# Releasing the software DMA loads at the first memset instead of at the first cast of q

## The chip, the cores and the metric

The kernel runs on one core of one Trainium2 chip. The metric is the time of the device for one execution, in microseconds, as the median of several runs. The profile is of one execution and has a span of its own (310.0 us here), a little apart from the median.

## The reference

The input is q, k and v of 4 batches, 8 heads, 768 positions and 64 elements per head, and a list of random blocks. Two stages follow each other.

```python
scores = scale * np.matmul(q, k.transpose(0, 1, 3, 2))
# mask: 32x32 blocks; neighbours, first and last row and column of blocks, 3 sampled blocks per row
scores = np.where(mask, scores, -1000000000.0)
attn = softmax(scores)
x = attn @ v                      # then heads side by side: (4, 768, 512)
...
a1 = alpha1 * x + beta1
tok = np.einsum('ts,bsd->btd', w_tok, a1)
u = x + lam * tok
a2 = alpha2 * u + beta2
ch = np.maximum(a2 @ w_ch1, 0.0) @ w_ch2
return u + lam * ch
```

The lines are shortened: the softmax subtracts the row maximum and adds a small constant to the sum. The second stage mixes tokens with a 768x768 matrix and then channels with a 512x2048 and a 2048x512 matrix, each time with a residual.

## The kernel before

**Tiling.** Heads are taken in 16 pairs, (batch, two heads). The scores of a pair are computed transposed, keys on partitions, in 9 units of 1,024 columns, so there are 144 units. For a unit, TensorE computes scores (L729 for the first 6 pairs, with the mask as 24 added rows of q and k; L850 for the rest, two heads side by side on half of the rows of the array), ScalarE takes the exponential into `eT` (L744, L802), and TensorE multiplies by v (L769, L883). The later pairs are masked after the exponential on VectorE (L807). A norm step (L701, L704) writes the result into `x_sb`. After both heads of a pair come the token mixing for the pair's 128 channels (L942 to L978, matmuls at L962) and a transpose into `uT` (L1000 and its copy for the first batch, a DMA transpose later). When a batch has all four pairs, channel mixing follows: `w1b` matmuls (L1044), a relu into `hts` (L1057, L1061), `w2b` matmuls (L1106), an add (L1123) and the store. The weights of the token mixing are transposed on TensorE at L506.

**Order of the work.** The start is written out by hand. The first pair's q and k (`q2f`, `k2f`), the identity for transposes, block indicators and sampled blocks come in on the queues of SyncE and ScalarE (L235 to L245). `warm` is a tile of zeros, set by VectorE at L248; `keep_warm` (L252) multiplies it by itself, so that TensorE isn't idle before the data is there. `first_cast(0)` turns q and k of the first head into bf16 in `rel0`; `transposes` (L294) and copies put them into `qx[0]` and `kx[0]`.

Everything else is ordered by a planner in the kernel's own code. Each piece of work is a `Job` with an engine, a duration, a priority and what it depends on. A loop walks through time, gives each free engine its best ready job, and emits the instruction at that moment. So each engine's instruction list is in the order of the planned times, and `pin_order` keeps it. The planned times are in no instruction: on the chip each engine runs its list in order and waits on semaphores only.

Five constants say where the plan begins. `T0` is the time from which TensorE, ScalarE, VectorE and SyncE are free for planned jobs (L59, L332); `POOL=4800.0` is the same for GpSimd; `dma_free` and `land.free`, both 8000, are the time from which the DMA engines can serve the software loads. A load is expected to land at `max(dma_free, issue + 2300)` plus its transfer time plus 200 (L1309 to L1311), one after the other.

```python
if e == "PE" and not st["ch2"]:
    fill(t - free_at[e] - 60.0)
```

These two lines (L1289, L1290) put fills into the list: where the plan has TensorE idle, up to the first job of the second channel matmul (L1106), `fill` emits matmuls of `warm` of about that length.

**The loads in question.** All casts during a load, that is q, k and v of later pairs and all weights, are issued by GpSimd (`load`, `load_wtk`, `load_bc`, `load_w1`, `load_w2`; L399 to L472), in the order of `LOADS`. Ahead of them stands one small copy on GpSimd (L324) that reads `rel0`. GpSimd runs in order, so no software load is issued before the first cast of q has written `rel0`.

Of the kernel before, what the change touches and what calls it, by code (L numbers as in the profile page):

```python
# [13 lines left out]
BF = mybir.dt.bfloat16  # L14
# [9 lines left out]
NBLK = S // BLK  # L24
# [3 lines left out]
P = 128  # L28
# [17 lines left out]
    "w1 3", "q 5", "k 5", "v 5", "q 6", "k 6", "v 6",  # L46
)
PR = 1
EARLY = ('b0', 'b1')
OLD = True  # L50
MROW = (2, 3, 9)
# [4 lines left out]
COVER = 800.0  # L56
NLD = 6
HOLD = 2
T0 = 6600.0  # L59
MASK_AT = 28  # L60
AHEAD = 13000.0
SCALE = 1.0 / 8.0
# [74 lines left out]
def kernel(  # L137
# [19 lines left out]
    nc = tc.nc  # L157
# [21 lines left out]
    pp = ctx.enter_context(tc.tile_pool(name="persist", bufs=1))  # L179
# [43 lines left out]
    def bank(name, shape, dt=FP):  # L223
        t = ps7[:, :] if name == "b6" else ps6[:, ts(ALL.index(name), 512)]
        if dt != FP:
            t = t.bitcast(dt)
        t = t[:, 0 : int(np.prod(shape[1:]))]
        return t if len(shape) == 2 else t.rearrange("p (o c) -> p o c", o=shape[1])
# [18 lines left out]
    warm = pp.tile([P, 512], BF, name="warm", tag="warm")  # L247
    nc.vector.memset(warm[:], 0.0)  # L248

    def keep_warm(n, w, name="b6"):  # L250
        for _ in range(n):
            nc.tensor.matmul(bank(name, [P, w]), warm[:, 0:P], warm[:, 0:w], start=True, stop=True)  # L252

    def fill(ns):
        free = [x for x in ("b6", "b0", "b1") if slots[x] > 0]
        while ns > 60.0 and free:
            w = min(512, int(ns * 2.4))
            keep_warm(1, w, free[0])
            ns -= w / 2.4 + 3.0

    keep_warm(7, 512)
    keep_warm(2, P)
    for t in vext:
# [16 lines left out]
    rel0 = wk.tile([P, 2, NT, 2 * D], BF, name="rel", tag="rel", bufs=3)  # L280
# [21 lines left out]
    for w in range(2):  # L302
# [12 lines left out]
        out=qx[0][MB, 0:HS], in0=bqs[0][0:NBLK, 0:HS], scalar1=1.0, scalar2=BIG,  # L315
# [4 lines left out]
    for j in range(2, NQB):  # L320
        nc.sync.dma_start(qx[j][MB, :], qx[0][MB, :])

    hold = pp.tile([P, NBLK], BF, name="hold", tag="hold")
    nc.gpsimd.tensor_copy(out=hold[:], in_=rel0[:, 0, 0, 0:NBLK])  # L324

    ACT_COPY = dict(ACT=790.0)
    dma_free = [8000.0]
    SEM = 70.0  # L330
    DRAIN = 166.0
    free_at = dict(NEVER=1e9, NONE=0.0, PE=T0, ACT=T0, DVE=T0, POOL=4800.0, SP=T0)  # L332
    slots = dict(
        **{b: 1 for b in ALL}, ops=1, eT=NET, head=NQB, vext=NV, ld=NLD, rel=3,
        x=NXB, uT=3, hts=2, a1p=2, ub=2, ot=2, w2b=1,
# [589 lines left out]
    for p in range(len(pairs)):  # L925
# [7 lines left out]
        halves = ((0, D), (D, D)) if n == NPAIR - 1 else ((0, P),)  # L933
        pr = PR if n == NPAIR - 1 else 2
        a_jobs = []
# [213 lines left out]
    def can(j):  # L1149
        for t in j.take:  # L1150
            if isinstance(t, tuple):
                opts = t[0]
                ok = False
                if opts is BANKS:
# [3 lines left out]
                    if st["qk"] < NPE * NU:  # L1158
                        opts = BANKS[:2] if st["ch"] else EARLY
                    elif not hold[1] and any(owned.values()):  # L1160
# [19 lines left out]
    hold = [False, False]  # L1180
# [43 lines left out]
            x[0].done = at + 200.0 + x[0].late  # L1224
        dma_free[0] = at

    land.free = 8000.0
    flying = []
    loads = sorted((j for j in jobs if j.xfer is not None), key=lambda j: (j.prio, j.n))
    t = 0.0  # L1230
# [165 lines left out]
```

The softmax here doesn't subtract the row's maximum and nothing guards it: scores larger than these inputs give would overflow.

## Time and profile before

| what | value |
|---|---|
| time, median of 3 runs | 309.87 us (309.76 to 309.95) |
| span of the profiled execution | 310.0 us |
| TensorE busy | 302.7 us (98%) |
| VectorE / ScalarE / GpSimd busy | 207.2 / 206.4 / 52.1 us |
| software queue: data, share of 16 DMA engines | 15.47 MB, 32.7% |
| first software load: issued, time to landing | 4.82 us, 4.2 us |
| first scores (L729) | 7.61 us |
| matmul records of `warm` after 13.4 us | 11, 3.76 us busy |

Busy time of TensorE is the union of its matmuls with their pipelined ends, so it can't tell a matmul that runs from one that waits for the one before it; starts of successive matmuls tell more. The chain that ended last is followed backwards from the end, at each step to what released the instruction. A name with a q (SPq, POOLq) is an engine's sequencer, which issues transfers. Some matmul records are missing: L252 has 36 matmuls on the program's list and 32 records in the trace.

### The profile page before, as it was taken

Reading aid. Unit: us, or ns where it says so; the run is one execution under the profiler, and the core shown is the slowest. Engines: PE = TensorE matmul, PEld = TensorE weight load, DVE = VectorE, ACT = ScalarE, POOL = GpSimd, SP = SyncE. Lnnn points to the kernel's source line nnn. Section 1 sums busy time; section 2 is a strip of 40 time slices with the busy share of each in tenths; the row PEclk is TensorE's granted clock in tenths of the full one; section 3 lists DMA queues with packets and bytes.
Section 4 is the critical chain, followed back from the end, with each engine's and each line's share of the span. In section 5 each row is a group of like instructions: output and inputs, shape, how many; then the busy total and the mean of one; then the engine's idle time right before and its main releaser. Section 6 shows DMA issues by size and latency. Waiting matters only on the chain.

```text
span 310.0 us, 7557 instructions
## 1 busy us (share of the span) xinstructions
PE 302.7 (98%) x3161; PEld 190.1 (61%) x3194; DVE 207.2 (67%) x435; ACT 206.4 (67%) x270; POOL 52.1 (17%) x91
## 2 busy tenths in 40 slices
PE   7999999999999999999999999999999999999995
PEld 3577788766655665565666575566655665555444
DVE  3379898988898886766889696888958730010111
ACT  4699998898798558756855767775858727428000
POOL 4736530301113112131211210120000000000000
PEclk9999999999999999999999999999999999999999
DMA  6999999995563757376285834558020110010121
GB/s 141 182 252 214 211 201 213 161 137 88 77 105 59 137 53 135 54 114 109 61 127 98 123 65 76 94 89 100 3 62 34 27 27 34 34 70 0 48 90 68
DMA packets 47174, 30.81 MB, mean 99 GB/s; under 512 B 27516, under 2 KB 43044, under 8 KB 47140
## 3 DMA queue, kind: packets, MB, share of 16 engines
q0 software_dynamic: 15984, 15.47, 32.7%
q1 hardware_dynamic: 30940, 14.61, 22.2%
q8 instruction: 25, 0.41, 0.6%
q10 hardware_dynamic: 216, 0.24, 0.3%
q14 instruction: 9, 0.07, 0.1%
HBM read 32.04 MB, written 6.33 MB: 124 GB/s over the span
## 4 chain that ended last, share of the span: by engine, by line
PE 95%; DMA 1%; ACT 1%; issue 1%; DVE 0%; SPq 0%
PE ps L1044 27%; PE ps L1106 21%; PE ps L962 10%; PE ps L729 8%; PE ops L883 8%; PE ps L850 7%; PE ops L1106 5%; PE ops L769 4%; PE ps L252 1%; PE ps L294 1%; DMA identb<-ident_c 1%; PE ps L506 1%; PE ps L1000 0%; ACT eT L802 0%; ACT hts L1057 0%
## 5 line engine op out<-in xcount | busy, mean ns | idle before, releaser
L802 ACT ACTIVATE eT<-ps 128x1024 f16<-128x1024 f32 x90 | 86.9, 1022 | 31.3 <-PE ps L850 27.3
L1044 PE MATMUL ps<-uT,w1b 128*128 128x384 bf16 (+1 forms) x512 | 93.1, 326 | 0.1
L1057 ACT ACTIVATE hts<-ps,b1t 128x384 bf16<-128x384 f32 x104 | 60.1, 582 | 37.7 <-PE ps L1044 32.2
L1106 PE MATMUL ps<-w2b,hts 128*128 128x512 bf16 (+1 forms) x293 | 72.4, 373 | 1.5 <-issue 0.2
L807 DVE TENSOR_TENSOR eT<-eT,maskT 128x1024 f16<-128x1024 f16 x90 | 60.3, 686 | 17.5 <-ACT eT L802 17.3
L1044 PEld LDWEIGHTS <-w1b 128*128 128x128 bf16 x512 | 46.3, 98 | 29.0 <-ACT eT L802 1.2
L1106 PEld LDWEIGHTS <-hts 128*128 128x128 bf16 x400 | 36.6, 98 | 36.2 <-issue 2.2
L744 ACT ACTIVATE eT<-ps 128x1024 f16<-128x1024 f32 (+1 forms) x55 | 52.6, 1016 | 7.1 <-PE ps L729 6.9
L883 PEld LDWEIGHTS <-eT 128*128 128x128 f16 x720 | 30.8, 97 | 15.1 <-issue 4.4
L962 PE MATMUL ps<-a1p,wtokT 128*128 128x128 bf16 x576 | 36.6, 219 | 0.0
L883 PE MATMUL ops<-vext,eT 128*128 128x65 f16 x720 | 36.0, 193 | 0.0
L962 PEld LDWEIGHTS <-wtokT 128*128 128x128 bf16 x576 | 33.3, 98 | 2.9 <-issue 0.5
L729 PE MATMUL ps<-qx,kx 88*128 88x512 bf16 (+1 forms) x144 | 33.2, 341 | 0.2 <-ACT kx L318 0.2
L1123 DVE TENSOR_TENSOR ot<-x_sb,ps 128x512 f32<-128x512 f32 (+1 forms) x20 | 13.4, 671 | 28.3 <-PE ps L1106 28.3
L397 POOL COPY held<-flag 1x1 bf16<-1x1 bf16 x24 | 9.4, 393 | 121.2 <-DVE flag L417 121.2
L850 PE MATMUL ps<-qx,kx 64*128 64x512 bf16 (+1 forms) x240 | 25.6, 326 | 0.0
L769 PEld LDWEIGHTS <-eT 128*128 128x128 f16 x432 | 18.6, 98 | 5.1 <-DVE x_sb L704 0.6
L769 PE MATMUL ops<-vext,eT 128*128 128x65 f16 x432 | 20.4, 194 | 0.1
L972 DVE TENSOR_TENSOR x_sb<-x_sb,ps 128x384 f32<-128x384 f32 x32 | 17.5, 549 | 3.9 <-PE ps L962 3.3
L704 DVE TENSOR_TENSOR x_sb<-ops,rcp 128x384 f32<-128x384 f32 x32 | 17.8, 557 | 1.1
L1123 DVE TENSOR_TENSOR ot<-x_sb,ops 128x512 f32<-128x512 f32 (+1 forms) x5 | 3.2, 634 | 22.5 <-PE ops L1106 22.5
L978 DVE TENSOR_TENSOR ub<-x_sb,a_bc 128x384 bf16<-128x384 f32 x32 | 17.6, 550 | 0.1
(68 smaller groups left out, 224.2 us busy)
## 6 DMA issues: line engine op xcount, KB each, us to landing
out_dram<-ot SPq DMA_DIRECT2D x23, 256.0 KB
v<-in_v_dram POOLq DMA_DIRECT2D x16, 192.0 KB, 4.5
q<-in_q_dram POOLq DMA_DIRECT2D x15, 192.0 KB, 3.9
k<-in_k_dram POOLq DMA_DIRECT2D x15, 192.0 KB, 4.7
w1b<-in_moe_w_ch_dram POOLq DMA_DIRECT2D x4, 512.0 KB, 9.2
w2b<-in_moe_w_ch_dram POOLq DMA_DIRECT2D x4, 512.0 KB, 11.8
wtk<-in_moe_w_tok_dram POOLq DMA_DIRECT2D x3, 384.0 KB, 9.2
maskT<-mask_rows SPq DMA_DIRECT2D x14, 72.0 KB
```

Of the source, the lines that this page charges most:

```text
L704: nc.vector.tensor_tensor(out=x_sb[:, s0 : s0 + NT, h * D : (h + 1) * D], in0=op[:, :, 0:D], in1=rcp[:].unsqueeze(2).broadcast_to([P, NT, D]),
L729: nc.tensor.matmul(sps[:, f - u * UN : f - u * UN + w], kx[h][0:KC, ts(jt, P)], qx[h][0:KC, c : c + w], start=True, stop=True,)
L744: nc.scalar.activation(eT[:, c], sps[:, c], AF.Exp, bias=EXPB, scale=SCALE)
L769: nc.tensor.matmul(ops[p, a][:, t * VW : t * VW + D + 1], eTs[p, u][:, ts(i - u * GU, P)], vx[:, a, jt, 0 : D + 1], start=(i % HT == 0), s ...
L802: nc.scalar.activation(eT[:], sps[:], AF.Exp, bias=EXPB, scale=SCALE)
L807: nc.vector.tensor_tensor(out=e, in0=e, in1=maskT[:, u, :].unsqueeze(1).broadcast_to([P, 2, 512]), op=ALU.min,)
L850: nc.tensor.matmul(sps[:, a * 512 + lo : a * 512 + lo + w], kx[sl][r, ts(jt, P)], qx[sl][r, c : c + w], start=True, stop=True,)
L883: nc.tensor.matmul(ops[p, a][:, t * VW : t * VW + D + 1], eTs[p, u][:, a * 512 + c * P : a * 512 + (c + 1) * P], vx[:, a, jt, 0 : D + 1], ...
L962: nc.tensor.matmul(tp[:, j, :], wtokT[:, s, ts(3 * g + j, P)], tl["a1p", p][:, s, :], start=(s == 0), stop=(s == NT - 1),)
L1044: nc.tensor.matmul(hp[:, 0:nc_], w1b[:, dk, ts(f, P)], uTs[b][:, dk, hf * HS : hf * HS + nc_], start=(dk == 0), stop=(dk == 3),)
L1057: nc.scalar.activation(hts[kk][:, f, :], hp[:, 0:HS], AF.Relu, bias=b1t[:, f : f + 1], scale=1.0)
L1106: nc.tensor.matmul(cps[kk, mi][:, 0:w], hts[kk][:, nk, ts(m, P)], w2tile[0][:, nk, lo : lo + w], start=(nk == 0), stop=(nk == 15),)
```

## The change

The copy on GpSimd that holds back the software loads now reads a piece of `warm`, so the loads are released when the first memset is done. It stands right after the memset in the program. The purpose is to have the loads under way while the first head's data still comes in. The planner's constants are set to go with that: GpSimd is free from 1500 instead of 4800, the DMA engines serve software loads from 4300 instead of 8000, and the other engines start planned jobs at 6200 instead of 6600. Rules, priorities and the order of the loads stay.

```diff
+DMA0 = 4300.0
+POOL0 = 1500.0
...
-T0 = 6600.0
+T0 = 6200.0
...
+    hold_ = pp.tile([1, 8], BF, name="hold", tag="hold")
+    nc.gpsimd.tensor_copy(out=hold_[:], in_=warm[0:1, 0:8])
     keep_warm(7, 512)
     keep_warm(2, P)
...
-    hold = pp.tile([P, NBLK], BF, name="hold", tag="hold")
-    nc.gpsimd.tensor_copy(out=hold[:], in_=rel0[:, 0, 0, 0:NBLK])
...
-    dma_free = [8000.0]
+    dma_free = [DMA0]
...
-    free_at = dict(NEVER=1e9, NONE=0.0, PE=T0, ACT=T0, DVE=T0, POOL=4800.0, SP=T0)
+    free_at = dict(NEVER=1e9, NONE=0.0, PE=T0, ACT=T0, DVE=T0, POOL=POOL0, SP=T0)
...
-    land.free = 8000.0
+    land.free = DMA0
```

## Prediction, made before the result was known

> **What bounds the kernel now.** I read the busy shares first, then the chain that ended last, then who waits, then the chain piece by piece. The page opens with the busy times and gives the chain by engine in its fourth part:
>
> ```profile
> PE 302.7 (98%) x3161; PEld 190.1 (61%) x3194; DVE 207.2 (67%) x435; ACT 206.4 (67%) x270; POOL 52.1 (17%) x91
> ...
> PE 95%; DMA 1%; ACT 1%; issue 1%; DVE 0%; SPq 0%
> ```
>
> TensorE is both the busiest engine and 95% of the chain. The busy figure is of pipelined matmuls, so I checked it with the waits of PE alone (us in total, times, longest):
>
> ```profile
> PE ps L252 <- DVE warm L248: 1.2, 1, 1.2
> PE ps L294 <- DMA identb<-ident_c: 0.4, 1, 0.4
> PE ps L729 <- ACT kx L318: 0.2, 1, 0.2
> ```
>
> All three lie in the first 8 us. After that PE runs its list with no wait over 0.2 us to the last matmul, which ends at 306.5; what follows is one add and a store. So the end time is a sum: the start, plus all matmuls on the list at their pace, plus 3.5 us of tail. Whatever is on the list counts in full, and that includes the fills of L252, matmuls of zeros that the planner emits where it thinks that PE would be idle.
>
> The pieces of the chain (start, length, what) give the pace:
>
> ```profile
> 1.69 3.28 DMA identb<-ident_c
> 5.00 0.80 PE ps L294 x6
> 7.61 1.87 PE ps L729 x5
> 10.12 1.01 PE ps L252 x3
> 11.12 0.85 PE ps L729 x3
> 11.98 0.85 PE ps L252 x2
> 40.91 0.87 PE ps L729 x5
> 299.57 3.45 PE ps L1106 x16
> ```
>
> The same five matmuls of L729 (2,048 columns) take 1.87 us at 7.61 and 0.87 us at 40.91: until about 13 us the array runs at half pace. At full pace 16 matmuls of 512 columns take 3.45 us, 0.421 ns per column; two fills of 512 at 11.98 take 0.85 us, twice that. The fills lie in the early part only. This is the table by stage for the instructions of `warm` alone (stretch, its length, PE busy and count):
>
> ```profile
> 13.40:60.00 46.60, 3.76 (x11) 1.38 (x15) 0.00 (x0) 1.00 1.16 210
> 60.00:310.00 250.00, 0.00 (x0) 0.00 (x0) 0.00 (x0) 1.00 0.43 76
> ```
>
> GpSimd, which issues the software loads, is held once at the start, and its first load follows at 4.82:
>
> ```profile
> POOL hold L324 <- DVE rel L289: 4.2, 1, 4.2
> ```
>
> No VectorE, ScalarE or PE instruction waits for a software load anywhere in the profile: the planner knows when they land, and places their readers later. So the loads bound nothing on the chip directly; they shape the order that the planner writes.
>
> **What the Trainium skill says.** "TensorE: Matmul & The Clock Gate", Part 1, has the array at half clock until a window of about 3.4 us has been busy throughout. The trace agrees on the ratio (1.87 against 0.87 us); with the gaps at 4.6 and 7.4 us full pace came only at 13.3. "DMA: Bandwidth & Descriptors", section "Issuing engines are not separate DMA queues", says that transfers from all issuing engines run on the same 16 DMA engines and interleave. The trace of before keeps them apart: software packets first show after 6.2 us, when the load issued at 4.82 begins to move. From 3 to 6.2 us the two hardware queues alone take 62.2% + 9.8% = 72% of the 16 engines. So the early release puts software traffic onto engines that are three quarters full.
>
> **The change, part by part.**
>
> 1. The copy on GpSimd that holds the loads reads `warm` instead of `rel0`. `warm` is set at 0.86 + 0.27 = 1.13 us, the cast ends at 4.54. The copy took 0.26 us, so the first issue moves from 4.82 to about 1.4: 3.4 us earlier. GpSimd is no bound (52 us busy), so this alone is worth nothing on the path.
>
> 2. Contention. Software data moved about 1.5 us after issue (4.82 to 6.2 or later), so now from about 3.0. The transfers for the first head are then still in flight: both casts start near 4.1, and `identb` lands at 4.97, which is what starts the transposes at 5.00. Bounds: nothing, if the hardware packets are nearly done; 0.9 us, if the last 0.9 us before 4.97 are shared evenly and take twice as long. The second halves of q and k are read at 7.30 and 7.58, and the transposes that need them start at 9.27, so about 1 us of delay there is hidden. I take 0.3 us for the start. It goes to the end in full, as PE has no later slack.
>
> 3. Loads land earlier. The total traffic is the same, and part of the 3.4 us is paid in shared time. Between 3 and 8 us before moved about 0.6 MB on hardware queues; 28% of the engines were free for 3.2 us, worth about 0.9 us of full use. So landings should move by 1 to 2.5 us, while the planner (`DMA0` 8000 to 4300) counts on 3.7. Does a reader stall? In the changed order the cast of the first v load follows the mask copy at 8.03 to 8.38. That load landed at 4.82 + 4.2 = 9.0 in before; moved by 1 to 2.5 us that is 6.5 to 8.0. First q: 5.66 + 4.4 = 10.1, now 7.6 to 9.1. First k: 6.37 + 5.6 = 12.0, now 9.5 to 11. Its cast is due after 10.1, so up to 0.9 us of VectorE wait, ahead of the copy of kx for the second head. That copy serves only the fifth unit, whose matmuls ran after 14 us. Hidden.
>
> 4. The constants `DMA0`, `POOL0` and `T0` make no instruction, but the planner writes another order. I compared the built lists. All work is the same: every line but L252 has the same count and shapes of matmuls, and the groups of L850 keep their number (35), so what changing over to them costs stays. The fills do not: before has 14,060 columns, after 19,092. The first 5,944 columns (the warming ones and the three fills at 10.12) are common. What is left: 8,116 in before, of which 1,024 at half pace (the 0.85 us at 11.98), so 7,092 x 0.421 = 2.99 us at full pace. In after 13,148, of which the first 507 fall in the half-pace time, so 12,641 x 0.421 = 5.32 us. Difference +2.33. In the half-pace time after has 517 columns of fill less, about 0.43 us of clock, in which real matmuls advance by half as much: -0.21. Net +2.1 us.
>
> Why more fills? With data there sooner, the token transposes (L506) and the token mixing (L962) move forward, but L1044, the large block of independent work, starts later in the sequence: after unit 49 instead of 45. Most of the added fills stand between units 37 and 48, where the list holds only scores, attention-times-v and little else. There ScalarE's exponentials, about 0.92 us apart in the trace, set the pace; scores and values of a unit need 0.44 + 0.24 us of PE. Whether PE waits there or multiplies zeros is the same for the end: it is PE time without work, and the last 50 us (256 to 306.5) are channel mixing that runs as fast as PE can. Being ahead with attention buys nothing there.
>
> 5. The hold tile shrinks and moves: nothing.
>
> Sum: 309.87 + 2.1 (fills) + 0.3 (start) = 312.3 us.
>
> **The rivals.**
>
> A. A new wait on top. A start later by 0.5 to 0.9 us can leave the window after 9.9 us not busy throughout, with full pace one window later: 3.4 us at half pace, 1.7 us lost. Or VectorE, in order, waits for loads that are 1 to 2 us later than planned and PE runs dry. Either gives about 314.0. For: landings fall short of the plan. Against: the margins of step 3.
>
> B. No change. The fills are paid, but full pace comes one window earlier, since real work reaches PE sooner: -1.7, so 309.87 + 2.1 - 1.7 = 310.3. Against: everything up to 10.9 us is the same sequence with the same gaps.
>
> C. Faster. The exponentials have 1.5 + 0.7 us of idle before the third and fourth unit (10.5 to 13.7); values multiplied early shorten it, and if ScalarE set the end, that would be 309.87 - 2.2 = 307.7. For: ScalarE is busy 43.0 of 46.6 us from 13.4 to 60. Against: PE has no wait there either, and work that it does not do then it must do later.
>
> **How the numbers follow.** The forecast has 0.68, A 0.15, B 0.10, C 0.07. The forecast itself has 310.9 (half of the added fills displace short waits that the lists hide, no contention) to 313.2 (0.9 at the start, a few short waits). The range 310.3 to 314.0 leaves out C and the far ends of A and B. Slower is the forecast and A, 0.83; B is within 0.2%, 0.10; C is faster, 0.07.
>
> **What would show it.** Right: some 30 fills after 13.4 us (before's list has 15), with about 2.3 us more of chain time; still no PE wait after 10 us; the first software issue near 1.4; identb landing between 5.0 and 5.9; last matmul near 309. Wrong: fills in place but the last matmul no later (then before had waits that I took for work), full pace well before 13 us, or PE waits of over 1 us after 14.

## The result, and the profile after

The changed kernel takes 317.71 us (median of 3 runs, 316.7 to 318.15) against 309.87 (309.76 to 309.95): a ratio of 1.0247 [1.0208, 1.0286], slower by 7.8 us. Measured again beside the kernel before (E1) it was 318.54 against 311.64, 1.022 [1.0192, 1.0247], slower by 6.9 us. The first three runs of before lie at the fast end of the 113 that followed (309.53 to 315.16), so the experiments below compare with that second pair. The direction was forecast; the size was 2.4 us, and 317.71 lies above the range. The profiled execution of the changed kernel has a span of 314.9 us (before: 310.0).

Busy times of the engines and the chain by engine, from the page of the kernel after:

```profile
PE 307.7 (98%) x3208; PEld 190.8 (61%) x3208; DVE 209.8 (67%) x438; ACT 204.0 (65%) x267; POOL 52.2 (17%) x91
...
PE 91%; ACT 3%; DMA 3%; DVE 1%; issue 0%; ACTq 0%
```

TensorE is as busy as ever, but its share of the chain fell from 95% to 91%. About 7% of the span now runs through ScalarE, VectorE and transfers, 2% before: time in which TensorE waits. The list of PE's waits (us in total, times, longest) shows only the first part of it:

```profile
PE ps L254 <- DVE warm L250: 1.2, 1, 1.2
PE ps L299 <- DMA identb<-ident_c: 0.9, 1, 0.9
PE ps L299 <- DVE rel L294: 0.7, 1, 0.7
PE ps L1047 <- ACT eT L805: 0.2, 1, 0.2
```

The wait for `identb` grew from 0.4 to 0.9 us, and one for the cast into `rel` is new. The first loads go out where they were meant to. GpSimd's instructions at the start (start, length, engine, line; in brackets the idle time and what ended it):

```profile
1.20 0.18 POOL L265 COPY hold<-warm 1x8 bf16<-1x8 bf16 x1 [0.75 <-DVE warm L250]
1.33 0.84 POOL L402 DMA_DIRECT2D v<-in_v_dram  x1
2.17 0.72 POOL L402 DMA_DIRECT2D q<-in_q_dram  x1
```

The first issue is at 1.33 instead of 4.82, and the first seven software loads land 1.5 to 2.4 us earlier (first v 6.66 instead of 9.02, first q 8.58 instead of 10.03). What it cost is in the chain of the first 15 us, piece by piece:

```profile
0.74 3.07 DMA q2f<-in_q_dram
...
3.83 6.34 DMA k2f<-in_k_dram
...
10.19 0.37 DVE rel L294
...
10.61 0.82 PE ps L299 x6
11.43 1.01 PE ps L254 x3
12.44 0.85 PE ps L732 x3
```

The chain now goes through the second half of the first pair's k. Its cast starts at 10.19, where before it started at 7.58, and the transposes of the second head start at 10.61 instead of 9.27. The two casts from the traces, first before, then after:

```profile
7.58 0.42 DVE L289 CAST rel<-k2f 128x384 bf16<-128x384 f32 x1
```

```profile
10.19 0.36 DVE L294 CAST rel<-k2f 128x384 bf16<-128x384 f32 x1 [1.90 <-DMA k2f<-in_k_dram]
```

Before, the data was there when VectorE came to it; now VectorE stands 1.90 us, and what follows on its list with it. The queues from 3 to 6.2 us in the kernel after (packets, MB, share of the 16 engines) say why:

```profile
q0 software_dynamic: 327, 0.24, 50.4%
q1 hardware_dynamic: 338, 0.23, 32.3%
```

SyncE's queue, which carries `k2f`, moved 588 packets and 0.56 MB in this stretch before, and 338 and 0.23 MB now. Software traffic had nothing there before, and has half of the engines now. ScalarE's queue has 14.2%, 9.8% before.

For the rest of the kernel I took the start of every matmul from the two traces and priced the work on the list at its full-pace length (0.421 ns per column and the like). What is left over is fills and a remainder, that is waits and half pace:

| us, in the profiled execution | before | after | difference |
|---|---|---|---|
| remainder at the first scores | 3.74 | 4.19 | +0.45 |
| remainder at the third unit's scores | 5.33 | 6.65 | +1.3 |
| remainder at the first scores of L850 / L853 (near 74 us) | 7.78 | 8.79 | +1.0 |
| remainder from there to the last matmul | 7.73 | 9.42 | +1.7 |
| all matmuls of `warm` on the list | 5.96 | 8.09 | +2.13 |
| start of the last matmul | 306.24 | 311.08 | +4.84 |

The remainder to 74 us (+1.0), the remainder after it (+1.7) and the fills (+2.1) make the 4.8 us. The fills are what was forecast. The other two parts were not, and the experiments are about them. The execution profiled in E1, with a span of 317.3, is closer to the median: there the remainder at 20 us is 2.55 us above before's (9.45 against 6.90), and the late one 2.2 us; its last matmul starts 7.2 us later than before's.

When full pace comes can be read from the lengths of equal matmuls and from the granted clock that each profile records: at 13.8 us in before (the prediction had read 13.3) and at 13.5 in after. So in this pair of profiles the longer pauses at the start are a cost, and a longer half pace is none.

### The profile page after: what moved, and what is told of

It reads as the page before. It is cut to its first block, busy times and chain, and to the rows that moved or that the text cites. A ratio compares the mean times of both kernels' runs of the same rounds, so it can differ in the third digit from the quotient of the medians.

```text
span 314.9 us, 7624 instructions
## 1 busy us (share of the span) xinstructions
PE 307.7 (98%) x3208; PEld 190.8 (61%) x3208; DVE 209.8 (67%) x438; ACT 204.0 (65%) x267; POOL 52.2 (17%) x91
## 4 chain that ended last, share of the span: by engine, by line
PE 91%; ACT 3%; DMA 3%; DVE 1%; issue 0%; ACTq 0%
PE ps L1047 27%; PE ps L1109 21%; PE ps L965 10%; PE ops L886 8%; PE ps L853 7%; PE ps L732 6%; PE ops L1109 5%; PE ops L772 4%; ACT eT L747 2%; DMA k2f<-in_k_dram 2%; PE ps L254 2%; DMA q2f<-in_q_dram 1%; PE ps L299 1%; ACT eT L805 1%; DVE ot L1126 1%; PE ps L509 1%
## 5 line engine op out<-in xcount | busy, mean ns | idle before, releaser
L1060 ACT ACTIVATE hts<-ps,b1t 128x384 bf16<-128x384 f32 x101 | 58.2, 583 | 43.7 <-PE ps L1047 37.2
L1109 PE MATMUL ps<-w2b,hts 128*128 128x512 bf16 (+1 forms) x320 | 76.5, 374 | 0.0
L810 DVE TENSOR_TENSOR eT<-eT,maskT 128x1024 f16<-128x1024 f16 x90 | 60.7, 686 | 16.8 <-ACT eT L805 16.7
L886 PEld LDWEIGHTS <-eT 128*128 128x128 f16 x720 | 30.2, 97 | 14.1 <-DVE eT L810 2.2
L886 PE MATMUL ops<-vext,eT 128*128 128x65 f16 x720 | 35.4, 193 | 0.2 <-DVE eT L810 0.2
L1126 DVE TENSOR_TENSOR ot<-x_sb,ps 128x512 f32<-128x512 f32 (+1 forms) x20 | 13.4, 672 | 29.8 <-PE ps L1109 29.7
L732 PE MATMUL ps<-qx,kx 88*128 88x512 bf16 (+1 forms) x144 | 32.7, 337 | 0.2 <-ACT kx L323 0.2
L853 PE MATMUL ps<-qx,kx 64*128 64x512 bf16 (+1 forms) x240 | 26.0, 326 | 0.0
L772 PEld LDWEIGHTS <-eT 128*128 128x128 f16 x432 | 18.2, 98 | 5.4 <-DVE x_sb L707 0.7
L1064 DVE TENSOR_SCALAR hts<-ps,b1t 128x384 bf16<-128x384 f32 x27 | 16.6, 616 | 5.0 <-PE ps L1047 3.7
L772 PE MATMUL ops<-vext,eT 128*128 128x65 f16 x432 | 19.9, 194 | 0.0
```

The costliest lines, as they stand in the source:

```text
L732: nc.tensor.matmul(sps[:, f - u * UN : f - u * UN + w], kx[h][0:KC, ts(jt, P)], qx[h][0:KC, c : c + w], start=True, stop=True,)
L772: nc.tensor.matmul(ops[p, a][:, t * VW : t * VW + D + 1], eTs[p, u][:, ts(i - u * GU, P)], vx[:, a, jt, 0 : D + 1], start=(i % HT == 0), s ...
L810: nc.vector.tensor_tensor(out=e, in0=e, in1=maskT[:, u, :].unsqueeze(1).broadcast_to([P, 2, 512]), op=ALU.min,)
L853: nc.tensor.matmul(sps[:, a * 512 + lo : a * 512 + lo + w], kx[sl][r, ts(jt, P)], qx[sl][r, c : c + w], start=True, stop=True,)
L886: nc.tensor.matmul(ops[p, a][:, t * VW : t * VW + D + 1], eTs[p, u][:, a * 512 + c * P : a * 512 + (c + 1) * P], vx[:, a, jt, 0 : D + 1], ...
L1060: nc.scalar.activation(hts[kk][:, f, :], hp[:, 0:HS], AF.Relu, bias=b1t[:, f : f + 1], scale=1.0)
```

## The experiments

Theory one: three costs add up. The early release slows the first head's loads, so TensorE pauses and is later at full pace; the new list has 2.1 us more of planned idle time; and the new list, of equal work, has late waits. Theory two, the rival: only the start counts (a pause, and half pace prolonged), and the order is worth its fills at most. A third: the fills themselves cost. Every run below is 5 to 22 executions beside the kernel before; medians of before are 311.64 to 311.9, and single executions of one kernel spread by 1 to 5 us. "The late remainder" is the remainder from the 24th matmul of L850 to the last matmul: 6.85 us in before, 8.54 in after. It belongs to the order, and not to the start: that stretch takes 218.8 us in before and in all seven other profiles with before's late order (E2, E5, E6, E9, E11, E12, E13), and 220.5 to 221.0 us in the five with after's order (after, E1, E3, E4, E8).

**E1: the changed kernel again.**

> The changed kernel once more, beside the kernel before on the same chip. The profiled spans differ by 4.9 us (310.0 and 314.9), the medians by 7.8 us. My account of the spans: 2.1 us of added fills, 1.0 us of a later start, 1.7 us of small waits of TensorE between 125 and 215 us. If the span tells the change, the time here is before + 5 us (ratio 1.016). If the medians do, it is before + 8 us (ratio 1.025), and 3 us more are to be found outside my account.

318.54 us, 1.022 [1.0192, 1.0247]. That lies between the two sizes that were weighed. The slowdown stands in a second measurement, and its profile shows how the start varies from run to run. Its chain:

```profile
11.86 1.01 PE ps L254 x3
12.87 0.85 PE ps L732 x3
...
14.58 0.85 PE ps L732 x3
```

Three matmuls of L732 take 0.85 us at 14.58, half pace; in the profile after they took 0.45 at 13.91. Full pace came at 13.5 us there, at 17.0 here, later than in before too.

**E2: the release alone.** The constants of before are put back, so all lists but GpSimd's copy are before's.

```diff
-DMA0 = 4300.0
-POOL0 = 1500.0
-T0 = 6200.0
+DMA0 = 8000.0
+POOL0 = 4800.0
+T0 = 6600.0
```

> The early release alone: the planner's three constants are those of before, and every engine's list is that of before but for the copy on GpSimd. Theory (the changed order costs most): only the start is later, identb 0.45 us and the second half of k another 0.6 to 0.9 us, so before + 1.0 to 1.3 us. Rival (contention costs most, all through the loads): before + 4 us or more. Third: the later half of k is hidden here and the time is before + 0.5 us or less.

313.35 us, 1.007 [1.0046, 1.0093]: +1.7, more than the 1.0 to 1.3 of the theory. The chain of its start:

```profile
3.68 6.93 DMA k2f<-in_k_dram
...
10.63 0.37 DVE rel L294
...
11.05 0.82 PE ps L299 x6
11.87 1.01 PE ps L254 x3
12.87 0.85 PE ps L732 x3
13.73 0.85 PE ps L254 x2
```

The same transfer ends the wait, with before's order of work. The pace is another than in after. The table by stage has the granted clock in the third column from the right:

```profile
4.80:8.20 3.40, 1.41 (x15) 0.81 (x14) 1.17 (x3) 1.30 (x3) 2.06 (x4) 1.00 1.14 202
8.20:15.00 6.80, 5.82 (x21) 2.73 (x22) 3.16 (x9) 3.26 (x5) 1.82 (x4) 0.50 1.21 220
```

Full pace was there from 4.8 us and was lost at 8.2, after pauses, until 15.0. The transposes of the second head start 1.8 us later than in before (11.05 against 9.27), and the 120th matmul of the first scores 1.5 us later (62.02 against 60.52): in this profile the later data is the whole cost, and pace adds nothing to it on balance. The late remainder is before's. So the release by itself costs a quarter of the slowdown, all of it at the start.

**E3: the order alone.** The lists of after, with the loads released by the first cast as before.

```diff
-    hold_ = pp.tile([1, 8], BF, name="hold", tag="hold")
-    nc.gpsimd.tensor_copy(out=hold_[:], in_=warm[0:1, 0:8])
...
+    hold_ = pp.tile([P, NBLK], BF, name="hold", tag="hold")
+    nc.gpsimd.tensor_copy(out=hold_[:], in_=rel0[:, 0, 0, 0:NBLK])
```

> The changed order alone: constants and lists of the changed kernel, but the copy on GpSimd reads rel0 after the first cast, as before. Theory: fills 2.1 us and the later waits 1.7 us stay, the start is that of before, so before + 3.8 us; loads that now land 1.5 to 2.5 us later than in the changed kernel add up to 1 us if a list runs into them. Rival (contention costs most): within 1 us of before.

317.99 us, 1.0197 [1.0168, 1.0227]: +6.35, more than expected. The order carries nearly all of it, but this run has a wait of its own, since the list counts on loads that now come late:

```profile
PE ps L297 <- DVE kx L367: 2.2, 1, 2.2
```

Full pace was there from 5.7 us, was lost at 12.6, after this wait, and came back at 19.4. The late remainder is 8.52, as in after: those waits belong to the order, not to the release. The costs of E2 and E3 don't add up to that of after (1.7 + 6.35 against 6.9): each changes the same start, and E3 has its own wait.

**E4: the order of after without fills.** Left out are only matmuls of zeros, which have no part in the result.

```diff
-                if e == "PE" and not st["ch2"]:
-                    fill(t - free_at[e] - 60.0)
```

> The changed kernel with the planner's fills left out (only the hand-written warming matmuls at the start stay); all other instructions and their order are the same. As I predicted: where fills stand TensorE would wait anyway, so it waits instead of multiplying zeros, and the time is the changed kernel's within 1 us. Rival (fills delay real work that was ready): up to 5.6 us less than the changed kernel, as that is the length of the fills left out, or at least the 2.1 us. Risk on the other side: a pause lets the array fall to half pace, and it is slower.

316.44 us, 1.0154 [1.0129, 1.0179]: 2.1 us less than after beside it, where within 1 us was expected and the rival had 2.1 or more. But the remainder grew as the fills went: at the 120th matmul of L732 fills and remainder make 16.24 us, against 16.72 in the profile after, and at the end 25.99 against 26.30 (28.70 in E1). Two of PE's waits:

```profile
PE ps L299 <- DVE rel L294: 3.2, 1, 3.2
...
PE ps L732 <- ACT eT L747: 2.2, 7, 0.4
```

TensorE waits for the exponentials where it multiplied zeros. From 20 us to the 120th matmul of L732, at full pace throughout, fills and remainder together take 5.1 us in E4 and 5.9 in after, E1, E3 and E8: of the 4.9 us of fills that stood there, 4.1 came back as waits. So the fills of the plan are for the most part idle time under another name, and some 0.8 us of them are a cost of their own. The rest of the 2.1 us lies ahead of 20 us or in chance: E4's start has full pace from 4.9 us and half pace from 11.7 to 15.1, and the changed kernel's has half pace to 13.5 or 17.0. How it divides is not shown. The third theory holds for a part at most.

**E5: is it one load?** The release alone, with the second half of k on ScalarE's queue, so that it needn't wait behind the others on SyncE's.

```diff
+    nc.scalar.dma_start(k2f[:, 1, :], pair_ap(k, 0, 0)[:, 1, :])
...
-    nc.sync.dma_start(k2f[:, 1, :], pair_ap(k, 0, 0)[:, 1, :])
```

> Early release with before's constants and order, and the second half of the first k issued on ScalarE's queue right after that queue's other loads, instead of as the sixth load on SyncE's. In the traces with early release that half lands at 10.2 us instead of by 7.6, and VectorE and then TensorE wait for it. Theory (this one late load is most of what the release costs): before + 0.5 us or less, where the release alone gave before + 1.7. Rival (the release slows all first loads, identb too, or disturbs the clock): still before + 1.2 us or more.

313.95 us, 1.0075 [1.0052, 1.0099]: +2.3, a miss. PE's waits, and VectorE's casts in the timeline:

```profile
PE ps L299 <- DMA identb<-ident_c: 1.8, 1, 1.8
PE ps L299 <- DVE rel L294: 1.6, 1, 1.6
```

```profile
11.10 0.36 DVE L294 CAST rel<-q2f 128x384 bf16<-128x384 f32 x1 [2.83 <-DMA q2f<-in_q_dram]
```

In E2 these two waits are 1.7 and 0.8 us. So `identb` is as late as there, and the second half of q is now the last to land, at 11.1, where in E2 it was k's at 10.6. The delay moved to another load. The release slows several of the first loads, and moving one to the other queue didn't help.

**E6, E7: the fills by size, with the release of before.** Only constants of the kernel before change. E6 plans 13,529 columns of fill (before: 14,060), E7 23,963.

```diff
-    dma_free = [8000.0]
-    land.free = 8000.0
+    dma_free = [7000.0]  # E6; E7: 8500.0
+    land.free = 7000.0   # E6; E7: 8500.0 and T0 = 6400.0
```

> Release as before; the planner's constants 7000 for the loads and 6600 for the engines, which give the fewest fill columns among the constants tried: 13,529, against 14,060 before and 19,092 after. Theory one (fills count what TensorE loses early): before - 0.2 us, plus or minus 0.3 for small waits. Theory two (any other order costs about 2 us in late waits, since the fine order of before happens to avoid them): before + 1.5 us or more.

> Release as before; constants 8500 and 6400, which give 23,963 fill columns, 9,903 more than before. Theory one: 9,903 x 0.421 ns = 4.2 us more, so before + 4.2 us, and before + 5.9 us if the late waits of 1.7 us come with it as they did in the changed order. Rival (fill columns have little to do with the time): within 1.5 us of before.

E6: 311.66 us, 0.9998 [0.9969, 1.0026], as expected. E7: 322.89, 1.0341 [1.03, 1.0381], +11.2 where 4.2 to 5.9 were expected. The trace of E7 has the fills at their price, 10.14 us against 5.96, so +4.2. The remainder is 6.8 us larger on top (22.27 against 15.51). The start isn't the reason, as full pace was there from 4.4 us; it was lost only from 62.5 to 65.9, right after the first of these waits of PE (58.7 to 61.8):

```profile
PE ps L294 <- DVE kx L363: 2.9, 1, 2.9
PE ps L962 <- DVE hts L1061: 1.2, 1, 1.2
```

As in after, a list of the same work has waits beside its fills. The fills show at face value in the trace; they don't tell the whole price of an order.

**E8, E9: the start's pauses closed.** E8 is after with two more warming matmuls before the first transposes and two before those of the second head. E9, the control, is before with one more at the start.

```diff
-    keep_warm(7, 512)
+    keep_warm(9, 512)   # E9: keep_warm(8, 512), and only that
...
+                keep_warm(2, 512)
                 tl["h0"] = transposes(
```

> The changed kernel with four more warming matmuls of 512 columns: two at the end of the first nine, where TensorE waits for identb, and two ahead of the transposes of the second head, where it waits for the second half of k. Theory (the pauses let the half pace last longer; in two profiles of the changed kernel full pace came at 13.5 and 17.0 us, with 2.4 us between the spans): 1 to 2 us faster than the changed kernel. Rival (pauses of 1 us do not matter to the clock, its moment is chance): the changed kernel's time within 0.4 us.

> The kernel before with one more warming matmul of 512 columns at the end of the first nine, where TensorE waits for identb (0.43 us at half pace). Control for the changed kernel with its pauses filled, which gained 2.7 us. If longer half pace is a cost of the change (its pauses are longer), before has little to win: 0 to 0.5 us faster. Rival (both kernels start equally cold, and filling would help either): before - 1.5 us or more, and then the clock explains nothing of the difference.

E8: 315.84 us, 1.0123 [1.0079, 1.0167], 2.7 us less than after, though it adds four matmuls. Zeros can't bring the data sooner, so this is won through the pace. The single executions say the same: four with a mean granted clock of 0.999 or 1.0 took 315.63 to 315.94 us, the two at 0.995 318.04 and 318.55. The profile is of the last, in which half pace came back from 13.4 to 16.8 us, so it doesn't show the gain. E9: 311.51, 0.9998 [0.9973, 1.0022], as expected, but for a reason that I had not foreseen. In its profile full pace is there at 5.35 us, and the kernel is 3.2 us ahead until 60 (the 120th matmul of L729 starts at 57.35 instead of 60.52). Then (waits of PE, and the chain from 63 us):

```profile
PE ps L850 <- DMA kx<-rel: 2.1, 1, 2.1
```

```profile
63.96 8.62 DMA kx<-rel
...
72.63 0.61 PE ps L850 x6
73.24 0.66 PE ops L769 x16
73.90 1.71 PE ps L1106 x4
```

The first pair of L850 can't start before its q and k have come through the loads and the DMA transposes. What was gained ahead of it is waited out there, and four matmuls of L1106 at 73.90 then take 1.71 us, half pace again. This is a second bound of before, hidden close behind the first. It also spoils the control: the start of before did gain from filling, as the rival had it, and the gain was waited out. So E8 shows that closing the pauses speeds up the changed kernel, and not that its half pace is longer than before's.

**E10: the same fills, another late order.** Constants 7000 and `T0` 6700 with the release of before: 13,529 columns as in E6, the order different from the first pair of L850 on.

> Release as before; constants 7000 and 6700: 13,529 fill columns, as few as in the run that equalled before, but a different order from the first masked pair on, where that run had before's own. Theory (in another order the late waits come to about 1.7 us, as in the changed kernel's): before + 1 to 2 us, from the stage after 75 us alone. Rival (only fills count): before - 0.2 us, within 0.3.

314.48 us, 1.0085 [1.0055, 1.0115]: +2.7, more than expected, and 2.8 us more than E6 beside equal fills. The late remainder is 8.84 (before 6.85), so late waits come with another order even without added fills or an early release. They are not the whole difference: between the 120th matmul of L729 and the 24th of L850 the remainder grows by 2.1 us more than in E6, and the start of this profile, with full pace at 10.5 us, is 1.6 us better. The waits of PE in E10:

```profile
PE ps L1044 <- ACT eT L802: 1.1, 2, 0.8
PE ops L769 <- DVE b1t L363: 0.9, 1, 0.9
PE ps L850 <- ACT eT L802: 0.3, 1, 0.3
```

In after, single late waits are too short for that list, but the chain from 75 to 252 us picks them up. By line, first E6 (before's late order), then after:

```profile
by line: PE ps L1044 31.9%; PE ps L1106 27.7%; PE ops L883 13.5%; PE ps L962 13.2%; PE ps L850 12.5%; ACT eT L802 0.6%; ACT hts L1057 0.4%; issue 0.2%; ACT b1t L361 0.1%
```

```profile
by line: PE ps L1047 33.9%; PE ps L1109 26.3%; PE ops L886 13.6%; PE ps L853 11.7%; PE ps L965 11.4%; ACT eT L805 1.2%; DVE ot L1126 0.8%; DVE eT L810 0.4%; DVE hts L1064 0.4%; issue 0.2%; PE ops L772 0.2%; DVE flag L420 0.0%; ACTq L805 0.0
```

ScalarE and VectorE have 1.1% of 177 us in E6 (1.9 us), and 2.8% in after (5.0 us): an exponential, a masking product, an add that frees a bank, each a link where TensorE found its next operand not ready.

**E11: the best of the constants, pause closed.** E6 with `keep_warm(8, 512)`.

> Candidate for the best: the order with 13,529 fill columns and before's late part, release as before, and the one warming matmul more at the start. Before - 0.2 us from the fills and 0 to -0.5 us from the clock: 0.2 to 0.7 us faster than before. The rival of the control would make it 1.7 us faster.

310.99 us, 0.9976 [0.9956, 0.9995]: 0.75 us less than before, about as expected. It beats both kernels, by little; the wait at the first pair of L850 stands at 2.5 us there.

**E12, E13: the release once the pauses are closed.** E12 is E2 with the four warming matmuls of E8, E13 is E12 with `DMA0 = 7000.0`.

> Early release with before's constants and order, and the same four warming matmuls as in the changed kernel with pauses filled. The release alone cost 1.7 us. Theory one (nearly all of it is the late landing of first loads, 1.3 us in the trace, which fills do not bring back): before + 1 to 1.5 us. Theory two (most of it is longer half pace): before + 0.5 us or less.

> Early release, the four warming matmuls, and the constants 7000 and 6600, which give 13,529 planned fill columns ahead of the four and before's own late order. What early release can be worth: with release as before and a fast start, TensorE waited 2.1 to 2.5 us for the transposed k of the first masked pair at about 70 us, as the loads were late; with early release it did not. Theory (loads then stop being the second bound): 0.5 to 1.5 us faster than before. Rival (the late landing of the first head's data eats that up): within 0.4 us of before, as the same start did with before's constants.

E12: 311.57 us, 1.0007 [0.998, 1.0034], where E2 had 1.007. The chain of its start:

```profile
3.95 6.06 DMA k2f<-in_k_dram
...
10.45 0.51 PE ps L299 x6
...
11.47 0.44 PE ps L733 x3
```

The transposes come 0.6 us sooner (10.45, E2 11.05), and TensorE is at full pace: 0.51 us for six transposes instead of 0.82. The wait at the first pair of L850 that E9 had is gone, since the loads are earlier. The median is theory two's. But the traces don't make the late data free of cost: E9 and E12 have the same order of work and full pace from 5.3 and 5.2 us, and the 120th matmul of the first scores starts at 57.35 us in E9 and at 59.53 in E12. So at equal pace the late data still costs 2.2 us there, a part of which the three more matmuls of zeros fill. This profile gains the pace, keeps the gain at L850 and ends 1.0 us ahead of before's; how the gain and the delay weigh in the median isn't shown. E13: 312.1, 1.0005 [0.9979, 1.003], where 0.5 to 1.5 us of gain were expected; the rival had it right. The early release wins nothing that these runs can tell from zero, even with the pauses filled and few fills.

## Why the prediction was right in direction and wrong in size

Forecast: 2.1 (fills) + 0.3 (start) = 2.4. Measured: 6.9 beside before. By the profile of E1 the sum is 2.1 (fills) + 2.5 (start and half pace, to 20 us) + 2.2 (late remainder) = 6.8, of the 7.2 us by which its last matmul starts later. Two steps failed: the start was priced at 0.3 us (step 2), and a new order of equal work at nothing (step 4).

1. *Release worth nothing by itself, first issue near 1.4.* 1.33, and none of the runs with the early release was faster than before. Right.

2. *Contention: 0.3 us, and "about 1 us of delay there is hidden".* This step failed: by itself the release cost 1.7 us (E2). `identb` came 0.46 us later in after (4.97 to 5.43), inside the bounds of 0 to 0.9, but the transposes that wait for it started 1.3 us later in E2 and E5 (6.32 and 6.30 against 5.00). And for the second halves I compared their delay with the slack and never worked out the delay. Software traffic took 50.4% of the engines from 3 to 6.2 us, and the cast of the second half of k, under way then, started 2.6 us later: more than the 1 us of slack. TensorE paused a second time, and the transposes of the second head came 1.3 us (after) to 1.8 us (E1, E2) later. What the pauses do to the pace comes on top and varies: full pace came at 13.5 us in after, as in before, and at 17.0 in E1, the "one window later" of rival A. The Trainium skill, "TensorE: Matmul & The Clock Gate", Part 1, says that the moment depends on a free-running window of about 3.4 us and differs from run to run; the two profiles, 3.5 us apart, agree. The arbitration was there to be read too: the Trainium skill, "DMA: Bandwidth & Descriptors", "Queues, rings and completion order", says that each engine goes round its queues packet by packet, so a third queue takes a share of engines that I had called three quarters full. The trace shows the shares, and not the turns: 72% for the hardware queues became 32.3% + 14.2%.

3. *Loads land 1 to 2.5 us earlier, and their readers don't stall.* Landings right (1.5 to 2.4). No wait of PE for a software load's reader shows at the start of after. The stall of VectorE was on the first pair's own load instead, and its other copies queued behind it.

4. *The planner's order: +2.1 us for fills.* The term was right, 2.13 measured, 31 fills in the records after 13.4 us where some 30 were expected. E4 confirmed that most of the fill time is idle time. The step's other half failed: *"All work is the same"*, therefore the rest of the list costs the same. I had read from before that PE runs its list without waits, and carried that over to a list I had not seen run. Equal matmuls in another order had 1.7 to 2.2 us more of late waits (after, E1, E3, E4, E8, and E10 with no more fills than before); every profile with before's late order was free of them.

5. *Rivals.* A named what E1 shows of the start, full pace one window later, but as an alternative of 0.15; it came together with a delay of the first data beyond A's 0.9 us, and with late waits that no rival had. B and C failed: full pace came no more than 0.3 us earlier, and work brought forward bought nothing.

The signs listed as "wrong" were partly blind: there was no single wait over 1 us after 14 us in the list, yet some 2 us of short ones. The starts of successive matmuls, and the chain by line in a late window, show what a list of waits with a floor leaves out.

Open: which property of an order makes the late waits. The runs show who ends them (exponentials, masking products, adds that free a bank), not why before's and E6's order avoids them; I did not move single jobs to find out. The split between pause and half pace at the start differs from execution to execution. Filling the pauses won 2.7 us (E8) and 1.8 us (E12 beside E2), but before gained as well at its start (E9), so how much of the release's cost is pace isn't shown.

## What to carry to other kernels

Price traffic that is moved ahead by what is in flight at that time, load by load, against the slack of each: here the first data had 1 us at most, and software loads took half of the engines from 3 to 6.2 us. When a planner rewrites a list, equal work is not equal time; take an allowance for waits of the new list from other orders of the same work (here the remainder grew by 0.3 us in E6 and by 6.8 us in E7). And close the pauses of the start before judging anything that shifts them, in both kernels: with four matmuls of zeros the release alone took 1.8 us less (E12), and one moved the start of before by 3.2 us (E9).

## What the runs showed of the hardware

Full pace of the array first came between 4.3 us (E5) and 17.0 us (E1), with pauses at the start of 0.2 to 3.2 us, and in eight of the fifteen profiles it was lost again: in E2 from 8.2 to 15.0, in E3 from 12.6 to 19.4, in E9, after a wait of 2.1 us in mid-kernel, from 73.6 to 77.0. Within a profile the changes lie 3.41 us or a multiple of that apart. My estimate of the idle time in each such stretch, from the starts and columns of the matmuls, sorts them: of those that end before the last matmul, every stretch at full pace with 2.0 us of idle time or more was followed by half pace (2.0 in E13, 2.1 in E3, 2.4 in E2 and E9, 2.8 in E7), and none with 1.8 us or less (1.8 in E12). E11's wait of 2.5 us lies across two stretches, with 1.1 and 1.7 us of idle time in them, and full pace stayed.

The mean granted clock of an execution doesn't show a late first full pace: before reads 1.00, though its matmuls run at half pace to 13.8 us, because the record begins with the first change. It does show half pace that comes back. Of the 113 executions of before in the experiments, 59 read 1.00 and took 311.2 us on average, and 29 read 0.995, which is one stretch of 3.41 us at half pace, and took 312.8.

And moving a load from one hardware queue to another while software traffic ran (E5) sped up none of the first loads on balance; it changed which of them was last.
